# Moving two output evictions to VectorE and easing the first convolution steps in a fused conv + squared-ReLU MLP kernel

## The chip, the core and the metric

The kernel runs on one core of a Trainium2 chip. The metric is the device time of one execution in microseconds (us), the median of several runs. PE is the matrix engine (TensorE), with PEld for its weight loads; DVE is VectorE, ACT is ScalarE, POOL is GpSimd, and SP is the engine that issues nearly all DMAs.

## The reference

The input is `x` of 8 sequences, 4096 tokens each, 192 features. A causal convolution of 7 taps per head (8 heads, 24 features each), with softmaxed taps, is followed by an MLP with a squared ReLU. The tokens of all sequences stand in one row of 32768.

```python
w = softmax(weight, axis=-1)                       # 8 heads x 7 taps
out = einsum('hk,bskhg->bshg', w, x_unf)           # causal, 6 zeros ahead of each sequence
h = out @ w_in                                     # 192 -> 2048
g = s * maximum(h, 0)**2 + b
y = g @ w_out                                      # 2048 -> 192
```

Weights arrive as 64-bit floats; the kernel keeps each operand as a high and a low 32-bit part (fp32r), so one product becomes three matmuls: high by high, high by low, low by high.

## The kernel before

**Tiling.** Tokens are cut into 32 superblocks `n` of 1024, each of two blocks `j` of 512. The 2048 hidden features are 8 pairs `p` of 256. A step `(n, j, p)` computes one pair for one block: `first` (L522) makes `h`, 18 matmuls on 64 rows each; `relu` and `square` (L543, L551) run on ACT; a cast to `qh` (L554) and a subtraction to `ql` (L559) run on DVE; `second` (L604) adds 20 matmuls into four accumulators. Matmuls on the upper and the lower 64 rows stand in turn, so that two of them can run side by side. The finished `qh`, `ql` wait in `queue`, so that `second` runs two steps behind `first` (LAG = 2). When a block's eighth pair is done, its sums are evicted (L634 and L637 on ACT, L638, L642 and L647 on POOL).

**Superblock 0** is different. There the two blocks run side by side while the weights are still being widened, `second_whole` (L569) uses all 128 rows, and its eviction (L585 to L593) makes `oA` (128 features) on ACT, `oC` (64 features) on ACT and `oB` from `oC` on DVE. `oC` has one buffer, so that the second block's `oC` waits for the first block's `oB`.

**Tokens.** The features that a superblock needs are prepared by a `Tokens` object (L130) as a chain of 28 parts: for block 0 the seven taps of features A (L161, L163 on DVE), a copy on ACT (L178), a subtraction on DVE with the swap of halves by two DMAs (L180, then L171 and L172 into `wA`); then the seven taps of features B for both blocks at once, `hiB` (L191), and one part per block of L195 and L196 on DVE into `tB`. Behind the second of these parts `swap` sends `tB` to `wB` by two DMAs. Last come the nine parts of features A of block 1. `first` reads `sA`, then `tB` and `wB`, then `wA`.

**Who does parts when.** `convolve(k)` (L708) does the next k parts of the coming tokens. It stops at the last tap of a convolution, and parts that are not done then are `owed` to the next call. In superblock 1, block 0, each step calls `convolve(3)`; in block 1, which also does the column sums for the bias (L494 to L500), `convolve(1)`; in superblock 2 three and two in turn; from superblock 3 on two. `finish` (L261) completes at the start of a block what its first step cannot do without. Behind the first step of superblock 2, `biases` (L506) makes the bias with four small matmuls (L512).

**What sets the order.** Superblock 0 is traced with `in_order`, which keeps the written order on DVE, ACT and PE. Behind that a scheduler places the instructions of each engine by priority and by its own estimate of when they are ready, and each engine then runs its list strictly in that order. `convolve` runs `behind` the DVE and ACT instructions traced before it.

Of the kernel before, what the change touches and what calls it, by code (L numbers as in the profile page):

```python
# [13 lines left out]
AF = mybir.ActivationFunctionType  # L14
ALU = mybir.AluOpType
# [22 lines left out]
def conv_attention_then_squared_relu_mlp(  # L38
# [23 lines left out]
    nc = tc.nc  # L62
# [15 lines left out]
    sb = const.tile([P, 1], F32, name="sb")  # L78
# [29 lines left out]
    def behind(*engines):  # L108
        return last_of(*engines)()
# [168 lines left out]
    def w_outA(part, f, rows=slice(0, P)):  # L278
        return W[rows, f // 2, part, CI + f % 2 * P :][:, 0:P]

    def w_outB(f, rows=slice(0, P)):
        return WB[rows, f // 2, f % 2, :]
# [196 lines left out]
    def column_sums(k):  # L479

        nonlocal sumA, sumB
        if k == 1:
            free = wordp.tile([P, CT, 2], I32, name="words").bitcast(F32)
            free = free.rearrange("p f w -> p (f w)")
            sumA = free[:, 0 : 4 * P].rearrange("p (h c) -> p h c", h=2)
            sumB = free[:, 4 * P : 4 * P + 5 * DB]
            nc.gpsimd.memset(sumB[:, 0:DB], 0.0)
        for o, w in (
            (sumA, W[:, k, :, CI:CB]),
            (sumB[:, DB:].rearrange("p (j d) -> p j d", j=2), WB[:, k, :, :]),  # L490
        ):
            before = W[:, 0, :, CI:CB] if o is sumA else WB[:, 0, :, :]
            before = before.bitcast(F32) if k == 1 else o
            nc.vector.tensor_tensor(o, before, w.bitcast(F32), op=ALU.add)  # L494
        if k == NPAIR - 1:
            a, b = sumA, sumB[:, DB:]
            nc.vector.tensor_tensor(a[:, 0, :], a[:, 0, :], a[:, 1, :], op=ALU.add)
            nc.vector.tensor_tensor(a[:, 0, 0:P], a[:, 0, 0:P], a[:, 0, P:], op=ALU.add)
            nc.vector.tensor_tensor(b[:, 0:P], b[:, 0:P], b[:, P:], op=ALU.add)
            nc.vector.tensor_tensor(b[:, 0:DB], b[:, 0:DB], b[:, DB:P], op=ALU.add)  # L500
# [5 lines left out]
    def biases():  # L506

        pb = ps_h.tile([P, 2, BLK], F32, name="h")
        for k, cols in enumerate((sumA[:, 0, 0:P], sumB[:, 0:P])):
            for i in range(2):  # L510
                r = slice(i * HB, (i + 1) * HB)
                nc.tensor.matmul(pb[:, i, k : k + 1], cols[r], bb[r], start=True, stop=True)  # L512
        nc.scalar.copy(bias[:, 0:2], pb[:, 0, 0:2])
        nc.vector.tensor_tensor(bias[:, 0:2], bias[:, 0:2], pb[:, 1, 0:2], op=ALU.add)
        nc.vector.tensor_copy(bias[0:DB, 2:3], bias[DB:P, 1:2])
        for o, to, k in unbiased:
            rows = slice(0, o.shape[0])
            nc.gpsimd.tensor_scalar(o, o, bias[rows, k : k + 1], None, op0=ALU.add)
            nc.sync.dma_start(to, o)


    def first(n, j, p, meanwhile=None):  # L522
        h = ps_h.tile([P, 2, BLK], F32, name="h")
        halves = [tok[n].half(j, i) for i in range(2)]

        def both(w, part, at, start, stop):

            for i in range(2):
                chunk = halves[i][at]
                rows = slice(i * HB, (i + 1) * HB)  # L530
                nc.tensor.matmul(  # L531
                    h[:, i, :], w_in(w, p, chunk[0], rows), chunk[part], start=start, stop=stop
                )

        for at in (0, 2, 1):
            both(0, 1, at, at == 0, False)
            both(0, 2, at, False, False)
            both(1, 1, at, False, at == 1)
            if meanwhile and at == 0:
                meanwhile()  # L540
        return h
# [6 lines left out]
    def squares(h, cast):  # L548
        return square(relu(h), cast)
# [7 lines left out]
    def lows(q, qh):  # L557
        ql = qs.tile([P, 2, BLK], F32R, name="ql")
        nc.vector.tensor_tensor(ql, q, qh.bitcast(F32), op=ALU.subtract)  # L559
        return qh, ql  # L560
# [3 lines left out]
    def accumulators(n, j, p):  # L564
        if p == 0:
            acc[n, j] = [ps_o.tile([P, BLK], F32, name=f"acc{k}") for k in (1, 2, 1, 2)[: 4 if n else 2]]
        return acc[n, j]

    def second_whole(n, j, p, qh, ql):  # L569


        a1, a2 = accumulators(n, j, p)
        for i in range(2):
            f = 2 * p + i
            st, sp = f == 0, f == NF - 1
            nc.tensor.matmul(a2, w_outB(f), qh[:, i, :], start=st, stop=False)  # L576
            nc.tensor.matmul(a2, w_outB(f), ql[:, i, :], start=False, stop=sp)  # L577
        for i in range(2):
            f = 2 * p + i
            st, sp = f == 0, f == NF - 1  # L580
            nc.tensor.matmul(a1, w_outA(1, f), qh[:, i, :], start=st, stop=False)  # L581
            nc.tensor.matmul(a1, w_outA(0, f), qh[:, i, :], start=False, stop=False)  # L582
            nc.tensor.matmul(a1, w_outA(0, f), ql[:, i, :], start=False, stop=sp)  # L583
        if p == NPAIR - 1:
            t0 = n * SUP + j * BLK  # L585
            oA = outs.tile([P, BLK], F32, name="oA")
            nc.scalar.activation(oA, a1, AF.Identity, scale=sb)
            oC = outs.tile([DB, BLK], F32, name="oC", bufs=1)
            nc.scalar.activation(oC, a2[DB:P, :], AF.Identity, scale=sb[DB:P])  # L589
            oB = outs.tile([P, BLK], F32, name="oB")[0:DB]  # L590
            nc.vector.scalar_tensor_tensor(
                oB, a2[0:DB, :], sb[0:DB], oC, op0=ALU.mult, op1=ALU.add
            )  # L593
            unbiased.append((oA, outT[0:P, t0 : t0 + BLK], 0))
            unbiased.append((oB, outT[P:D, t0 : t0 + BLK], 2))
            del acc[n, j]
# [100 lines left out]
    def start_tokens(n):  # L697
        if n < NSUP:
            tok[n] = Tokens(n)
            tok[n].load()  # L700
# [7 lines left out]
    def convolve(k):  # L708


        k += owed[0]
        with behind(nc.vector, nc.scalar):
            while k and coming[0] in tok:
                try:
                    stop = next(tok[coming[0]].todo)
                except StopIteration:
                    coming[0] += 1
                    continue
                k -= 1
                if stop:  # L720
                    break
        owed[0] = k if coming[0] in tok else 0
# [38 lines left out]
    with in_order(nc.vector, nc.scalar, nc.tensor):  # L761
        with in_order(nc.sync):
            head()
        headed = last_of(nc.sync)
        for p in range(NPAIR):
            if p > 1:
                if p + 3 < NPAIR:
                    with headed():
                        fetch(p + 3)
                pair(p)  # L770
            if p > 0 and p not in TWICE:
                while len(queue) > (LAG if p < NPAIR - 1 else 0):
                    second_whole(*queue.pop(0))
# [3 lines left out]
    for n, j, p in steps:  # L777
        if p == 0:
            tok[n].finish(j)
            if j == 0:  # L780
                with headed():
                    start_tokens(n + 1)
            else:
                tok.pop(n - 1)
        with begun() if n == 1 else ExitStack():
            h = first(n, j, p)
            queue.append((n, j, p, *lows(*squares(h, nc.vector.tensor_copy))))
        if (n, j) == (1, 1):
            if p < NPAIR - 1:
                with behind(nc.vector):  # L790
                    column_sums(p + 1)
            convolve(1)
        elif p < NPAIR - 1 or n == 1:

            convolve(3 if n == 1 else 3 - p % 2 if n == 2 else 2)
        if (n, j, p) == (2, 0, 0):
            biases()


        while queue and len(queue) > LAG + (queue[0][2] == 0 and queue[0][:2] != (1, 0)):  # L800
            item = queue.pop(0)
            (second if item[0] else second_whole)(*item)
# [46 lines left out]
```

## Time and profile before

| | us |
|---|---|
| median of 3 runs | 2234.77 |
| range of the runs | 2234.75 to 2234.77 |
| span of the profiled execution | 2232.9 |
| PE busy in it | 2226.4 |
| of it without PE in the first 32 us | 1.55 |
| of it without PE from 2225 to the end | 4.5 |
| DVE busy | 1753.5 |
| ACT busy | 1286.4 |
| POOL busy | 317.8 |

The profile is one execution; its span runs from the first to the last instruction, and the medians above hold some 1.9 us more that lies around the span. Its own time beside the runs is that span. A matmul on 64 rows is shown as lasting 386 ns, but two of them run side by side and the next pair starts before the last has ended, so that positions are read from start to start: a step of superblock 1 or later takes 4.31 us on PE. The granted TensorE clock of the execution is 1.000 of 2.4 GHz.

### The profile page before, as it was taken

To read this page: it belongs to the slowest core of one execution; us is meant where nothing else is said; L and a number is where in the kernel's file an instruction comes from. 1 tells how busy PE (TensorE), PEld (TensorE's weight loads), DVE (VectorE), ACT (ScalarE), POOL (GpSimd) and SP (SyncE) were. 2 spreads that over 40 slices of the span, in tenths; PEclk is the share of its full clock that TensorE was granted. 3 is DMA by queue.
4 is the path that set the end of the run, shared out by engine and by line. 5 is a ranking of instruction groups with operands and counts; after the bars stand their busy time and mean duration, and the time that the engine had idled before them with its cause. 6 is when DMAs were issued, how large, how long until landed. Compare 5 with 4: busy or idle time off the path is not lost.

```text
span 2232.9 us, 45081 instructions
## 1 busy us (share of the span) xinstructions
PE 2226.4 (100%) x19330; PEld 1829.1 (82%) x19330; DVE 1753.5 (79%) x1995; ACT 1286.4 (58%) x1410; POOL 317.8 (14%) x205
## 2 busy tenths in 40 slices
PE   9999999999999999999999999999999999999999
PEld 6788888888888888888888888888888888888887
DVE  8898778777787787777877878778777787787764
ACT  8755555655555555555555555555655555556554
POOL 0022101111011011110110111111101111011110
PEclk9999999999999999999999999999999999999999
DMA  5113112121121111211111111112121121111110
GB/s 180 34 43 87 40 46 62 48 58 44 44 58 53 53 44 45 56 53 53 43 51 50 53 53 53 48 43 62 51 55 44 44 58 53 53 44 42 46 39 17
DMA packets 46168, 117.51 MB, mean 53 GB/s; under 512 B 7760, under 2 KB 8016, under 8 KB 45968
## 3 DMA queue, kind: packets, MB, share of 16 engines
q1 hardware_dynamic: 45824, 114.50, 18.6%
q8 instruction: 151, 2.47, 0.5%
q14 instruction: 49, 0.40, 0.1%
q10 hardware_dynamic: 144, 0.13, 0.0%
HBM read 31.64 MB, written 25.17 MB: 25 GB/s over the span
## 4 chain that ended last, share of the span: by engine, by line
PE 98%; DVE 1%; ACT 1%; DMA 0%; issue 0%; SPq 0%; DVEq 0%
PE acc L614 50%; PE h L531 46%; DVE accA L163 0%; PE acc L576 0%; ACT q L552 0%; DVE ql L559 0%; PE acc L577 0%; PE acc L583 0%; PE acc L582 0%; PE acc L581 0%; ACT qh L554 0%; ACT q L545 0%; DMA xA<-in_xA 0%; DVE t L315 0%; ACT oC L589 0%
## 5 line engine op out<-in xcount | busy, mean ns | idle before, releaser
L545 ACT ACTIVATE q<-h 128x1024 f32<-128x1024 f32 x512 | 525.5, 1026 | 902.8 <-PE h L531 900.4
L559 DVE TENSOR_TENSOR ql<-q,qh 128x1024 fp32r<-128x1024 f32 x512 | 656.7, 1283 | 56.3 <-ACT qh L554 2.6
L554 DVE CAST qh<-q 128x1024 fp32r<-128x1024 f32 x497 | 370.1, 745 | 395.7 <-ACT q L552 393.3
L614 PE MATMUL acc<-qh,W 64*128 64x512 f32 x3960 | 609.9, 386 | 0.0
L552 ACT ACTIVATE q<-q 128x1024 f32<-128x1024 f32 x512 | 543.6, 1062 | 15.9
L614 PEld LDWEIGHTS acc<-qh,W 64*128 64x128 f32 x3960 | 370.9, 184 | 77.9
L531 PE MATMUL h<-sA,W 64*128 64x512 f32 x3072 | 432.4, 387 | 0.0
L531 PE MATMUL h<-wA,W 64*128 64x512 f32 x3072 | 431.6, 386 | 0.0
L531 PE MATMUL h<-tB,W 64*128 64x512 f32 x1536 | 429.9, 386 | 0.0
L531 PE MATMUL h<-wB,W 64*128 64x512 f32 x1536 | 429.9, 386 | 0.0
L614 PE MATMUL acc<-ql,WB 64*128 64x512 f32 x1980 | 385.7, 386 | 0.4 <-DVE ql L559 0.4
L614 PE MATMUL acc<-qh,WB 64*128 64x512 f32 x1980 | 385.6, 386 | 0.0
L614 PE MATMUL acc<-ql,W 64*128 64x512 f32 x1980 | 385.5, 386 | 0.0
L638 POOL TENSOR_TENSOR oB<-oB,oB 128x512 f32<-128x512 f32 x61 | 115.2, 1889 | 1672.7 <-ACT oB L637 1672.7
L163 DVE SCALAR_TENSOR_TENSOR accA<-xA,tap,accA 128x512 f32<-128x512 f32 x378 | 341.5, 903 | 6.8
L531 PEld LDWEIGHTS h<-sA,W 64*128 64x128 f32 x3072 | 287.3, 184 | 62.9 <-issue 1.1
L531 PEld LDWEIGHTS h<-wA,W 64*128 64x128 f32 x3072 | 287.8, 184 | 60.4
L531 PEld LDWEIGHTS h<-tB,W 64*128 64x128 f32 x1536 | 282.6, 184 | 40.5 <-issue 0.2
L531 PEld LDWEIGHTS h<-wB,W 64*128 64x128 f32 x1536 | 282.5, 184 | 20.1
L614 PEld LDWEIGHTS acc<-ql,WB 64*128 64x128 f32 x1980 | 185.5, 184 | 40.1 <-DVE ql L559 1.3
L614 PEld LDWEIGHTS acc<-ql,W 64*128 64x128 f32 x1980 | 185.5, 184 | 39.0
L614 PEld LDWEIGHTS acc<-qh,WB 64*128 64x128 f32 x1980 | 185.5, 184 | 38.8
(115 smaller groups left out, 1035.4 us busy)
## 6 DMA issues: line engine op xcount, KB each, us to landing
wA<-sA SPq DMA_DIRECT2D x126, 256.0 KB, 3.6
outT<-oA SPq DMA_DIRECT2D x63, 256.0 KB, 2.0
wB<-tB SPq DMA_DIRECT2D x60, 256.0 KB, 3.4
xA<-in_xA SPq DMA_DIRECT2D x24, 515.0 KB, 3.6
xB<-in_xB SPq DMA_DIRECT2D x32, 259.0 KB, 2.6
oC<-oB SPq DMA_DIRECT2D x61, 128.0 KB, 2.2
outT<-oC SPq DMA_DIRECT2D x60, 128.0 KB, 2.3
words<-in_w SPq DMA_DIRECT2D x7, 768.0 KB, 6.2
```

Of the source, the lines that this page charges most:

```text
L163: nc.vector.scalar_tensor_tensor(acc, src, w[:, k : k + 1], acc, op0=ALU.mult, op1=ALU.add)
L531: nc.tensor.matmul(h[:, i, :], w_in(w, p, chunk[0], rows), chunk[part], start=start, stop=stop)
L545: nc.scalar.activation(q, h, AF.Relu)
L552: nc.scalar.activation(q, q, AF.Square)
L554: cast(qh, q)
L559: nc.vector.tensor_tensor(ql, q, qh.bitcast(F32), op=ALU.subtract)
L614: nc.tensor.matmul(accs[to + 2 * i], w(f, r), q[r, f % 2, :], start=start and f == 0, stop=stop and f == ends[i],)
L638: nc.gpsimd.tensor_tensor(o[1], o[1], o[3], op=ALU.add)
```

## The change

Two edits. In `second_whole`, `oA` of both blocks of superblock 0 is computed by DVE (`tensor_scalar`, out of the accumulator) in place of ACT. In superblock 1, block 0, the first step asks `convolve` for 0 parts and the second for 2, where each asked for 3.

```diff
@@ -584,7 +584,7 @@
         if p == NPAIR - 1:
             t0 = n * SUP + j * BLK
             oA = outs.tile([P, BLK], F32, name="oA")
-            nc.scalar.activation(oA, a1, AF.Identity, scale=sb)
+            nc.vector.tensor_scalar(oA, a1, sb, None, op0=ALU.mult)
             oC = outs.tile([DB, BLK], F32, name="oC", bufs=1)
@@ -792,7 +792,8 @@
         elif p < NPAIR - 1 or n == 1:
 
-            convolve(3 if n == 1 else 3 - p % 2 if n == 2 else 2)
+            ahead = (0, 2) if n == 1 else ()
+            convolve(ahead[p] if p < len(ahead) else 3 if n == 1 else 3 - p % 2 if n == 2 else 2)
```

The first condition above this branch is `(n, j) == (1, 1)`, so the two smaller numbers hold for block 0 of superblock 1 alone. Everything behind them moves by the parts that were not done.

**DVE from the end of superblock 0 on.** `acc_376` and `acc_388` are the features-A sums of blocks 0 and 1, `acc_377` and `acc_389` their features-B sums. Before:

```order
L216 TENSOR_TENSOR wB<-accB,hiB 64x512
L591 SCALAR_TENSOR_TENSOR oB<-acc_377,sb,oC 64x512
L591 SCALAR_TENSOR_TENSOR oB<-acc_389,sb,oC 64x512
L554 CAST qh<-q 128x1024
L559 TENSOR_TENSOR ql<-q,qh 128x1024
L216 TENSOR_TENSOR tB<-accB,hiB 64x512
L161 TENSOR_SCALAR accA<-xA,tap 128x512
L163 SCALAR_TENSOR_TENSOR accA<-xA,tap,accA 128x512 x2
```

Now:

```order
L216 TENSOR_TENSOR wB<-accB,hiB 64x512
L587 TENSOR_SCALAR oA<-acc_376,sb 128x512
L591 SCALAR_TENSOR_TENSOR oB<-acc_377,sb,oC 64x512
L587 TENSOR_SCALAR oA<-acc_388,sb 128x512
L591 SCALAR_TENSOR_TENSOR oB<-acc_389,sb,oC 64x512
L554 CAST qh<-q 128x1024
L559 TENSOR_TENSOR ql<-q,qh 128x1024
L216 TENSOR_TENSOR tB<-accB,hiB 64x512
```

The two evictions stand between those that DVE did before, and the taps L161 and L163 that followed L216 stand one step later.

**DVE at the end of superblock 1**, in steps (1,1,6) and (1,1,7), from the last of the column sums (L500) to the bias (L514). Before:

```order
L500 TENSOR_TENSOR words<-words 128x64
L163 SCALAR_TENSOR_TENSOR accA<-xA,tap,accA 128x512
L554 CAST qh<-q 128x1024
L559 TENSOR_TENSOR ql<-q,qh 128x1024
L514 TENSOR_TENSOR bias<-bias,h 128x2
```

Now:

```order
L500 TENSOR_TENSOR words<-words 128x64
L195 CAST tB<-accB 64x512
L196 TENSOR_TENSOR tB<-accB,hiB 64x512
L554 CAST qh<-q 128x1024
L559 TENSOR_TENSOR ql<-q,qh 128x1024
L514 TENSOR_TENSOR bias<-bias,h 128x2
```

Before, L163 stands once more between L559 and L514; now L195 and L196 stand there once more, for block 1. The features B of superblock 2 are thus split in the last two steps of superblock 1, four steps later than before, and the swap into `wB` follows the second pair.

**PE in the first step of superblock 2**, `first(2,0,0)` with the bias matmuls (L512) and `second(1,1,6)` (L614), each with the semaphore that it waits for (DMAHW is a DMA, DVE and Activation are engines). Before:

```order
L531 MATMUL h<-tB,W 128x512
L531 MATMUL h<-wB,W 128x512 [waits DMAHW7_49]
L531 MATMUL h<-wB,W 128x512 [waits DMAHW0_49]
L531 MATMUL h<-tB,W 128x512 x2
...
L531 MATMUL h<-wA,W 128x512 x4
L512 MATMUL h<-bb,words 128x1 [waits DVE_49,Activation_49]
...
L614 MATMUL acc_1515<-qh,WB 128x512
```

Now:

```order
L531 MATMUL h<-tB,W 128x512 [waits DVE_49]
L512 MATMUL h<-bb,words 128x1 [waits Activation_49]
...
L614 MATMUL acc_1504<-qh,WB 128x512
...
L614 MATMUL acc_1504<-ql,WB 128x512
L531 MATMUL h<-wB,W 128x512 [waits DMAHW7_49]
L614 MATMUL acc_1506<-ql,WB 128x512
...
L614 MATMUL acc_1503<-ql,W 128x512
L531 MATMUL h<-wB,W 128x512 [waits DMAHW0_49]
L531 MATMUL h<-tB,W 128x512 [waits DVE_49]
...
L531 MATMUL h<-wA,W 128x512 x4
L614 MATMUL acc_1505<-ql,W 128x512
```

The first seven matmuls of `second(1,1,6)` now stand ahead of the first matmul that reads `wB`, six more ahead of the second one, and the last seven behind the end of `first(2,0,0)`. This is the only place where the order of PE differs. From superblock 3 on, DVE runs one part behind where it stood before: a step that held L191 and one pair of L195 and L196 now holds L191 and both pairs, with a lighter step ahead of it.

## Rows read from the trace of the kernel before

**Rows 1.** Span and granted clock; then one window: its length, busy us (instructions), PEclk, DMA.

```profile
core 0: 2232.9 us, clock 1.000
...
106.30:1200.00 1093.70, 1093.70 (x9656) 903.96 (x9654) 871.66 (x982) 619.62 (x669) 166.35 (x104) 1.00 0.19 52
```

**Rows 2.** Timeline, superblock 1's start: start us, us, engine, line, operation, count, [idle, releaser].

```profile
91.54 0.69 ACT L587 ACTIVATE oA<-acc,sb 128x512 f32<-128x512 f32 x1
91.55 0.74 DVE L591 SCALAR_TENSOR_TENSOR oB<-acc,sb,oC 64x512 f32<-64x512 f32 x1 [1.32 <-ACT oC L589]
92.32 0.69 ACT L589 ACTIVATE oC<-acc,sb 64x512 f32<-64x512 f32 x1
92.37 0.85 PE L531 MATMUL h<-sA,W 64*128 64x512 f32 x6
93.03 1.02 ACT L545 ACTIVATE q<-h 128x1024 f32<-128x1024 f32 x1
95.91 1.23 DVE L559 TENSOR_TENSOR ql<-q,qh 128x1024 fp32r<-128x1024 f32 x1
96.45 0.39 PE L614 MATMUL acc<-qh,WB 64*128 64x512 f32 x2
97.19 0.50 PE L614 MATMUL acc<-ql,WB 64*128 64x512 f32 x2 [0.35 <-DVE ql L559]
99.36 0.84 PE L531 MATMUL h<-sA,W 64*128 64x512 f32 x6
100.59 1.23 DVE L559 TENSOR_TENSOR ql<-q,qh 128x1024 fp32r<-128x1024 f32 x1
104.05 0.84 PE L531 MATMUL h<-sA,W 64*128 64x512 f32 x6
```

**Rows 3.** Timeline, the last B part and its swap in the kernel before, step (1,1,3).

```profile
143.29 0.42 DVE L195 CAST tB<-accB 64x512 fp32r<-64x512 f32 x1
143.74 0.46 SPq L172 DMA_DIRECT2D wB<-tB  x1
144.46 0.46 SPq L171 DMA_DIRECT2D wB<-tB  x1
144.47 0.70 DVE L554 CAST qh<-q 128x1024 fp32r<-128x1024 f32 x1
146.41 0.69 DVE L494 TENSOR_TENSOR words<-words,W 128x512 f32<-128x512 f32 x1
```

**Rows 4.** Those two DMAs, L172 then L171, by line; then all 64 into wB.

```profile
DMA to landing us min/median/max: 3.1/3.1/3.1
...
DMA to landing us min/median/max: 3.5/3.5/3.5
...
DMA to landing us min/median/max: 2.2/3.3/4.7
```

**Rows 5.** Timeline, the first step of superblock 2.

```profile
155.27 0.74 DVE L163 SCALAR_TENSOR_TENSOR accA<-xA,tap,accA 128x512 f32<-128x512 f32 x1
156.41 0.39 PE L531 MATMUL h<-tB,W 64*128 64x512 f32 x1
157.77 0.50 PE L512 MATMUL h<-bb,words 64*128 64x1 f32 x8
158.13 0.48 PE L614 MATMUL acc<-qh,WB 64*128 64x512 f32 x2
160.54 0.84 PE L531 MATMUL h<-sA,W 64*128 64x512 f32 x6
```

**Rows 6.** Timeline, steady state: step (n,1,2) in a later superblock.

```profile
413.61 1.22 DVE L559 TENSOR_TENSOR ql<-q,qh 128x1024 fp32r<-128x1024 f32 x1
416.90 0.39 PE L614 MATMUL acc<-ql,WB 64*128 64x512 f32 x2
```

**Rows 7.** Groups by form in the first 18 us: line, operation, shape, count | busy us, mean ns.

```profile
L257 PE MATMUL acc<-xB,q 128*128 128x512 f32 x14 | 6.2, 596 | 0.0
L388 PE MATMUL acc<-q 128*128 128x512 f32 x2 | 2.1, 1142 | 1.0 <-POOL xA L145 1.0
```

## The prediction

> **What bounds the kernel now.** I read the busy times first: PE works in 2226.4 of 2232.9 us, with a granted clock of 1.000, the full 2.4 GHz, and behind 106.3 us without any gap (the order of the window's columns is PE, PEld, DVE, ACT, POOL) [rows 1]. So an edit on ACT or DVE pays only where PE waits for them. Of the 6.5 us without PE, 1.55 lie in the head and 4.5 in the tail, behind the last matmuls; the change touches neither. The second view was the timeline where superblock 1 begins. There `second(1,0,0)` puts its first `qh` pair on PE at 96.45 and its first `ql` pair only at 97.19, released by the DVE subtraction L559 that ran from 95.91 to 97.14; a second L559 ends at 101.82 and holds `second(1,0,1)` in the same way [rows 2]. These two are the waits that the change can take away. The third view was the timeline at the first step of superblock 2, where PE runs without a gap from 156.41 to 160.54 [rows 5], and the fourth the DMAs that carry `tB` to `wB` [rows 3, 4]; the order of the changed kernel shows that these two meet.
>
> **The rate of PE.** From the matmul at 156.41 to the bias at 157.77 there are 12 matmuls in 1.36 us [rows 5]: 0.113 us each when two row halves stand in turn, 0.227 a pair. A `first` of 18 is then 2.04 us, a `second` of 20 is 2.27, and a step 4.31.
>
> **Part 1, what the two waits are worth.** From 96.45 to 99.36 PE spends 2.91 us on a `second` that costs 2.27: 0.64 lost. From 99.36 to 104.05 it spends 4.69 on a step of 4.31: 0.38 lost [rows 2]. The most that can come back is 1.02 us. Behind them PE has no gap [rows 1].
>
> *The evictions.* ACT did `oA`, `oC`, `oA`, `oC` ahead of the first L545, 0.71 us apart, so from about 90.12 on, and L545 started at 93.03 [rows 2]. Without the two `oA` the first `oC` ends at 90.8. DVE now does `oA` ahead of its L591. No row shows this operation on DVE. One-input work on 512 columns takes 0.42 us (L195) [rows 3], the two-input L591 takes 0.74 us from an accumulator [rows 2]; I take 0.74, because L591 reads what `oA` reads, and 0.42 as the other end. PE ends the sums of block 1 near 90.25, block 0's are done before, so the first `oA` runs to about 91.0, the first `oB` to 91.75, the second `oC`, which waits for it, to 92.45. L545 cannot start before `first(1,0,0)` is through, and the next `first` started at 92.37 [rows 2], so its result is there at about 92.55. L545 thus comes 0.45 earlier than 93.03, limited by PE and no longer by ACT; with 0.42 for `oA` the limit is the same. The first L559 then ends at 97.14 - 0.45 = 96.69 where PE asks for it at 96.45 + 0.23 = 96.68. The 0.64 is gone but for about 0.07.
>
> *The smaller numbers.* Between the two subtractions DVE did L216 and three taps. The taps now stand a step later, which takes some 2 us out from ahead of the second L559, and the 0.38 is gone too. I take **0.95 us** back; the ends are 0, if a new wait takes the place of the old, and 1.02.
>
> *What is late instead.* Four parts fewer are done, and everything behind stands four parts later. The parts of superblock 1's own block 1 end one step later, some 4 us, and `first(1,1,0)` that reads them comes at about 121: covered by several us. The loads that SP issues behind released buffers (`xA`, `xB`) move behind the output DMAs, but they fetch a superblock ahead: nothing. The B split of superblock 2 has no such cover.
>
> **Part 2, the swap in front of superblock 2.** In the kernel before, the last B part began at 143.29 in step (1,1,3), and `first(2,0,0)` read `wB` at about 156.6: 13 us of cover. Now the same part is the last thing of step (1,1,7), and the cover is gone. I place it on the clock of before. DVE's first pair L195, L196 stands where L163 started, at 155.27 [rows 5]. From there to the next cast is 144.47 - 143.29 = 1.18 us, and through cast and subtraction 146.41 - 144.47 = 1.94 [rows 3]: the second pair starts at 155.27 + 3.12 = 158.39. SP issued L172 0.45 and L171 1.17 behind the start of that pair [rows 3]: 158.84 and 159.56. These two DMAs took 3.1 and 3.5 us to land [rows 4]: 161.94 and 163.06. The 64 into `wB` lie between 2.2, which are the half-sized ones, and 4.7 [rows 4]; I take the pair's own.
>
> PE reaches the first `wB` matmul early: 156.41, plus 0.23 for the single `tB` matmul, plus 0.36 for the bias (157.77 to 158.13), plus seven matmuls of `second(1,1,6)` at 0.33 (the first pair is slower there) + 0.23 + 0.23 + 0.23 [rows 5]: 158.02. It waits until 161.94, **3.92 us**. Behind that stand this matmul, alone since the next is on the same rows, and six more: 0.23 + 3 x 0.23 = 0.91, to 162.85, and the second `wB` matmul waits 0.21 for L171, to 163.06. Ten matmuls end `first(2,0,0)` at 164.2, seven end `second(1,1,6)` at 165.0, and the next `first` can pair with the last of them, so 164.95 where it was 160.54 [rows 5]: **4.4 us** later. Of this 4.13 is waiting, the rest matmuls whose partner on the other rows is missing. The scheduler's filling is counted: without the thirteen matmuls moved forward the wait would be longer. Nothing hides the rest, since PE's list is strict. ACT and DVE idle meanwhile and start behind it with less backlog than before; POOL's six bias additions follow L514, which is late by 0.3 us at most.
>
> **Part 3, the steady state.** One step of each later superblock holds L191 and both pairs of L195 and L196, in place of L191 and one pair. That is one pair more, 1.18 us [rows 3]; the step ahead is lighter by about that. L559 ended at 414.83 where PE asked at 416.90: 2.1 us of slack [rows 6]. I cost it at nothing; if the pair fell into POOL's work, which stretches DVE, it might take twice as long and would still fit.
>
> **The sum.** 2232.9 - 0.95 + 4.4 = 2236.4 us of span, so with the 1.87 us around it 2238.2, or 3.45 us (0.15%) above the median of 2234.77. Some 0.2%, 4.47 us, is what a measurement of this kernel can tell from no change, so 2238.2 counts as the same, though close to its edge at 2239.2. Ends: the gain 0 to 1.02; the DMAs 0.4 earlier to 1 later. This gives 2237.4 to 2240.1 on its own.
>
> **The rivals.**
>
> *PE's clock falls in the wait (slower).* The longest idle stretch of PE between head and tail is the 0.35 us at 97.19, and the clock is granted in full [rows 1, 2]; the new one is 3.9 us, and no row shows what PE does after such a one. At the very start, after no work at all, a matmul of 128x512 took 1142 ns where the same shape took 596 ns a little later, with the granted clock still shown as 1.000 [rows 1, 7]. Half speed for as long as those two matmuls lasted, 2.1 us [rows 7], would cost 1 us, for four times that 4 us; I take twice, 4.2 us, so 2.1 lost: 2238.2 + 2.1 = 2240.3, with ends at 2239.2 and 2242.4. It decides by the length of the gap: 0.35 us leaves the clock alone, and if it falls only in a gap of more than 3.9 us nothing happens. The Trainium skill ("TensorE: Matmul & The Clock Gate", section "HAM oscillation — how this bites in real kernels") says that an engine idle for too long between bursts restarts at half clock; no run here shows it, and the time would be the one just given.
>
> *The swap is hidden after all (no wait).* If DVE is ahead of PE there and the pair starts some us earlier than I place it, the wait shrinks by the same. For: DVE's load in block 1 is smaller now. Against: the cast between the two pairs needs ACT's square of (1,1,7), and with it PE's own position, so that not much over 1 us can be won. Without any wait: 2233.8; with 1 us won: 2237.2.
>
> *A step of every superblock overruns (slower).* From 2.1 us more than I count, each of some 29 superblocks would lose the excess: 0.2 us each is 5.8 us, 2244. The lighter step ahead speaks against it.
>
> *The change does not do what it says.* DVE's `oA` sits in front of `oB`, on which the second `oC` waits; were it to take over 1.2 us, L545 would be as late as before. The taps' part of the gain stays: 2238.8.
>
> **How the numbers follow.** The forecast, a wait of about 4 us at the full clock: 0.60. The clock falls: 0.20. A wait shorter by over 1 us: 0.13. The steady state: 0.04. Evictions no help: 0.03, inside the forecast's range. The range reaches from the shorter wait to the fallen clock, 2236.0 to 2241.5. Slower by over 0.2% are the fallen clock, the steady state and the upper end of the forecast: 0.20 + 0.04 + 0.08 = 0.32. Faster by over 0.2% would need 4.47 us, of which the waits hold 1.02: 0.01. The same: 0.67.
>
> **What would show it.** Right: no `ql` wait left in `second(1,0,0)`; L587 on DVE near 0.7 us; PE waiting once for about 3.9 us at a `wB` matmul of `first(2,0,0)`, released by the DMA; 34.45 us from block to block behind it as before. Wrong: 64-row matmuls longer than 386 ns behind the wait (the clock), a wait under 3 us, or PE waiting again in the blocks behind.

## The result, and the profile of the changed kernel

The changed kernel takes **2240.26 us** (median of 12 runs, 2239.70 to 2241.38) against 2234.82 us of the kernel before on the same chip (2234.46 to 2235.05): a ratio of 1.0025, 95% interval 1.0017 to 1.0033. It is slower by 5.44 us, 0.24%. That lies inside the range that was forecast, 2.1 us above its centre and just beyond the 0.2% up to which "the same" was to go. The time is that of the rival in which PE's clock falls in the new wait.

The runs with a mean granted clock of 0.999 took 2239.70 to 2240.42 us, those with 0.998 took 2240.56 to 2241.38. Only the slowest of them was profiled (2241.38 us), so that its loss is read 1.1 us larger than the median's.

The span and the granted clock, which was 1.000 in [rows 1]:

```profile
core 0: 2239.6 us, clock 0.998
```

The one wait of PE that is new, from the view of waits (us in total, times, longest):

```profile
PE h L531 <- DMA wB<-tB: 3.9, 1, 3.9
```

Where PE stands idle and at which clock, by windows (length, busy us of PE, PEld, DVE, ACT, POOL with their counts, PEclk, DMA share, GB/s):

```profile
160.00:161.00 1.00, 0.00 (x0) 0.00 (x0) 0.00 (x0) 0.00 (x0) 1.00 (x2) 0.69 0.90 193
161.00:167.00 6.00, 5.45 (x26) 4.34 (x28) 0.00 (x0) 1.18 (x2) 6.00 (x4) 0.50 0.47 156
167.00:168.00 1.00, 1.00 (x12) 0.81 (x10) 0.07 (x1) 0.90 (x1) 1.00 (x2) 0.90 0.34 76
...
170.00:1200.00 1030.00, 1030.00 (x9092) 851.27 (x9090) 801.10 (x905) 585.11 (x630) 162.95 (x94) 1.00 0.19 52
1200.00:2190.00 990.00, 990.00 (x8738) 818.23 (x8736) 758.21 (x853) 562.23 (x605) 153.79 (x90) 1.00 0.18 49
```

Two losses stand behind each other: a wait of 3.9 us, and some 6.8 us at the lower of the two clock levels, 1.2 GHz. From 161.55, where PE works again, to 167.2 are 5.65 us of work at half rate, which at 2.4 GHz would have been 2.8. Behind 168 PE is busy in every microsecond at the full clock, with as many matmuls in each window as before (8738 in the second one in both kernels). The first of the two windows in the kernel before:

```profile
170.00:1200.00 1030.00, 1030.00 (x9090) 851.27 (x9090) 811.89 (x902) 582.40 (x628) 150.27 (x96) 1.00 0.19 52
```

**The head of superblock 1**, in the timeline (start us, us, engine, line, operation, count, [idle, releaser]):

```profile
90.42 0.69 ACT L589 ACTIVATE oC<-acc,sb 64x512 f32<-64x512 f32 x1
90.44 0.74 DVE L587 TENSOR_SCALAR oA<-acc,sb 128x512 f32<-128x512 f32 x1
90.52 0.97 PE L531 MATMUL h<-sA,W 64*128 64x512 f32 x6
91.98 0.69 ACT L589 ACTIVATE oC<-acc,sb 64x512 f32<-64x512 f32 x1 [0.87 <-DVE oB L591]
92.92 1.03 ACT L545 ACTIVATE q<-h 128x1024 f32<-128x1024 f32 x1 [0.25 <-PE h L531]
95.79 1.23 DVE L559 TENSOR_TENSOR ql<-q,qh 128x1024 fp32r<-128x1024 f32 x1
96.80 0.39 PE L614 MATMUL acc<-qh,WB 64*128 64x512 f32 x2
97.07 0.19 PEld L614 LDWEIGHTS acc<-ql,WB 64*128 64x128 f32 x2 [0.31 <-DVE ql L559]
97.08 0.50 PE L614 MATMUL acc<-ql,WB 64*128 64x512 f32 x2
99.25 0.84 PE L531 MATMUL h<-sA,W 64*128 64x512 f32 x6
103.56 0.84 PE L531 MATMUL h<-sA,W 64*128 64x512 f32 x6
```

In [rows 2] L545 stood behind ACT's evictions; here it waits for PE. The `ql` pair comes 0.28 us behind the `qh` pair (0.74 there), though its weight load (PEld) still waits 0.31 us for L559, and the next step takes 4.31 us (4.69 there). In the kernel before `first(1,0,0)` started at 90.17; from there to the matmul at 104.05 are 13.88 us, here 103.56 - 90.52 = 13.04. The change gives back **0.84 us**. (The start itself is 0.35 us later in this profile: the head's matmuls took longer, and the change touches none of them.)

**The swap in front of superblock 2** in the timeline, with DVE, SP's queue and PE:

```profile
157.30 0.39 PE L614 MATMUL acc<-ql,WB 64*128 64x512 f32 x1
157.97 0.42 DVE L195 CAST tB<-accB 64x512 fp32r<-64x512 f32 x1
158.42 0.46 SPq L172 DMA_DIRECT2D wB<-tB  x1
159.14 0.46 SPq L171 DMA_DIRECT2D wB<-tB  x1
161.55 0.79 PE L531 MATMUL h<-wB,W 64*128 64x512 f32 x1 [3.86 <-DMA wB<-tB]
163.00 0.62 PE L531 MATMUL h<-wB,W 64*128 64x512 f32 x1
166.41 0.62 PE L531 MATMUL h<-sA,W 64*128 64x512 f32 x1
```

The two DMAs, by line of the tile `wB`:

```profile
DMA to landing us min/median/max: 3.1/3.2/3.4
```

Where [rows 3] have this cast at 143.29, it now starts at 157.97, and its two DMAs land 3.1 and 3.4 us behind their issue (3.1 and 3.5 in [rows 4]). Matmuls that last 0.39 us elsewhere last 0.62 here, at the granted clock of 0.50.

### The profile page after: what moved, and what is told of

Same layout as the page of the kernel before. It is cut to its first block, busy times and chain, and to the rows that moved or that the text cites. A ratio compares the mean times of both kernels' runs of the same rounds, so it can differ in the third digit from the quotient of the medians.

```text
span 2239.6 us, 45098 instructions
## 1 busy us (share of the span) xinstructions
PE 2230.3 (100%) x19330; PEld 1831.9 (82%) x19330; DVE 1727.6 (77%) x1997; ACT 1288.4 (58%) x1408; POOL 337.8 (15%) x205
## 4 chain that ended last, share of the span: by engine, by line
PE 99%; DVE 0%; DMA 0%; ACT 0%; issue 0%; DVEq 0%; POOL 0%; POOLq 0%
PE acc L614 50%; PE h L531 47%; PE acc L257 1%; PE acc L576 0%; PE acc L577 0%; PE acc L583 0%; PE acc L582 0%; PE acc L581 0%; PE acc L388 0%; DMA wB<-tB 0%; DVE ql L559 0%; DVE qh L554 0%; ACT q L552 0%; ACT q L545 0%; DVE words L494 0%
## 5 line engine op out<-in xcount | busy, mean ns | idle before, releaser
L545 ACT ACTIVATE q<-h 128x1024 f32<-128x1024 f32 x512 | 526.1, 1027 | 902.0 <-PE h L531 899.8
L614 PE MATMUL acc<-qh,W 64*128 64x512 f32 x3960 | 860.9, 387 | 0.0
L559 DVE TENSOR_TENSOR ql<-q,qh 128x1024 fp32r<-128x1024 f32 x512 | 664.1, 1297 | 55.5 <-ACT qh L554 2.6
L614 PEld LDWEIGHTS acc<-qh,W 64*128 64x128 f32 x3960 | 632.8, 184 | 78.2
L614 PE MATMUL acc<-ql,W 64*128 64x512 f32 x1980 | 676.2, 386 | 0.0
L531 PE MATMUL h<-sA,W 64*128 64x512 f32 x3072 | 650.0, 387 | 0.0
L531 PE MATMUL h<-wA,W 64*128 64x512 f32 x3072 | 649.8, 387 | 0.0
L614 PE MATMUL acc<-ql,WB 64*128 64x512 f32 x1980 | 570.0, 386 | 0.0
L614 PE MATMUL acc<-qh,WB 64*128 64x512 f32 x1980 | 569.4, 386 | 0.0
L531 PE MATMUL h<-wB,W 64*128 64x512 f32 x1536 | 509.1, 387 | 3.9 <-DMA wB<-tB 3.9
L531 PEld LDWEIGHTS h<-sA,W 64*128 64x128 f32 x3072 | 460.8, 184 | 63.0 <-issue 1.5
L531 PEld LDWEIGHTS h<-wA,W 64*128 64x128 f32 x3072 | 461.6, 184 | 60.6
L531 PE MATMUL h<-tB,W 64*128 64x512 f32 x1536 | 508.1, 386 | 0.0
L614 PEld LDWEIGHTS acc<-ql,W 64*128 64x128 f32 x1980 | 359.8, 184 | 39.1
L163 DVE SCALAR_TENSOR_TENSOR accA<-xA,tap,accA 128x512 f32<-128x512 f32 x378 | 341.7, 904 | 6.8
L531 PEld LDWEIGHTS h<-tB,W 64*128 64x128 f32 x1536 | 282.5, 184 | 40.5 <-issue 0.2
L614 PEld LDWEIGHTS acc<-ql,WB 64*128 64x128 f32 x1980 | 272.6, 184 | 39.2 <-DVE ql L559 0.3
L614 PEld LDWEIGHTS acc<-qh,WB 64*128 64x128 f32 x1980 | 272.4, 184 | 38.8
L531 PEld LDWEIGHTS h<-wB,W 64*128 64x128 f32 x1536 | 282.9, 184 | 24.5 <-DMA wB<-tB 4.3
```

What stands on the lines that cost most here:

```text
L163: nc.vector.scalar_tensor_tensor(acc, src, w[:, k : k + 1], acc, op0=ALU.mult, op1=ALU.add)
L531: nc.tensor.matmul(h[:, i, :], w_in(w, p, chunk[0], rows), chunk[part], start=start, stop=stop)
L545: nc.scalar.activation(q, h, AF.Relu)
L614: nc.tensor.matmul(accs[to + 2 * i], w(f, r), q[r, f % 2, :], start=start and f == 0, stop=stop and f == ends[i],)
```

## The experiments

The theory: the whole loss is the swap, which now ends in step (1,1,7); it costs a wait, and the wait costs the clock. The evictions and the taps at the head are harmless and give back 0.84 us. The rivals: the evictions on VectorE, or the later superblocks, carry a part of the loss; and the slow matmuls behind the wait come from something other than PE's standing idle. The kernel before took 2234.84 to 2234.89 us (median) beside all of these.

### Each half of the change alone

The evictions alone:

```diff
-            ahead = (0, 2) if n == 1 else ()
+            ahead = ()
```

> VectorE does the two features-A evictions of superblock 0, and the steps of superblock 1 do as many parts of the convolution as before. Theory (the whole loss is PE's wait for wB in first(2,0,0) and the low clock behind it; the evictions are harmless): the first ql wait is gone, the second stays, since the taps stand where they stood, and the B split stays in step (1,1,3), so no wB wait and no lower clock: some 0.5 us faster than before, 2234.3. Rival (the oA on VectorE costs something by itself, or the changed eviction leaves ACT and VectorE worse off behind it): no gain, 2235 or more.

The parts alone:

```diff
-            nc.vector.tensor_scalar(oA, a1, sb, None, op0=ALU.mult)
+            nc.scalar.activation(oA, a1, AF.Identity, scale=sb)
```

> The other half alone: the two evictions are on ACT as before, and superblock 1's first two steps do 0 and 2 parts. Theory: the wB wait of 3.9 us in first(2,0,0) and the stretch at half clock behind it are there in full, the first ql wait of 0.35 stays, the second is gone: some 0.4 us above the changed kernel, 2240.7 (2240.0 to 2241.9), by about 6 us slower than before. Rival (the loss needs the evictions on VectorE): 2234 to 2235, no wB wait.

The evictions alone: **2234.39 us**, ratio 0.9998 (0.9989 to 1.0006). The interval does not tell that from the kernel before, but the trace tells where it is gained: from 90.47 to 103.86 are 13.39 us, 0.49 less than the 13.88 of before. The parts alone: **2241.61 us**, ratio 1.0029 (1.0018 to 1.0039), a bit above what was expected, with a mean clock of 0.998 in five of its seven runs. Its head takes 104.06 - 90.52 = 13.54, 0.34 less than before. The timeline of the parts alone:

```profile
97.56 0.50 PE L614 MATMUL acc<-ql,WB 64*128 64x512 f32 x2 [0.38 <-DVE ql L559]
104.06 0.84 PE L531 MATMUL h<-sA,W 64*128 64x512 f32 x6
162.02 0.79 PE L531 MATMUL h<-wB,W 64*128 64x512 f32 x1 [3.83 <-DMA wB<-tB]
```

The first `ql` wait belongs to the evictions and the second to the taps, 0.49 and 0.34, together 0.83 of the 0.84. The wait at `wB` is there in full with all the evictions on ACT. The rival that VectorE's evictions cost something falls.

### All four parts given back (repaid)

```diff
-            ahead = (0, 2) if n == 1 else ()
+            ahead = (0, 2, 4, 4, 4, 4) if n == 1 else ()
```

> The changed kernel, but the four parts that the first two steps leave out are done by the four steps behind them (parts per step 0, 2, 4, 4, 4, 4, then 3): the B split of superblock 2 ends in the steps around (1,1,3) again. Theory: both ql waits are gone as in the changed kernel, no wB wait, clock 1.000: 0.85 us faster than before, 2234.0, and 6.3 us faster than the changed kernel. Rival (the loss comes from the order of the first superblock or from each later superblock): it stays at 2238 or more.

Measured **2233.89 us** (2233.52 to 2234.43), ratio to the kernel before 0.9996 (0.9987 to 1.0005): by the medians 0.95 us faster than before and 6.4 us faster than the changed kernel. Its clock is 1.000, and its `wB` matmuls follow `tB` at once:

```profile
155.10 0.84 PE L531 MATMUL h<-sA,W 64*128 64x512 f32 x6
155.78 0.39 PE L531 MATMUL h<-tB,W 64*128 64x512 f32 x1
155.78 0.61 PE L531 MATMUL h<-wB,W 64*128 64x512 f32 x2
159.91 0.84 PE L531 MATMUL h<-sA,W 64*128 64x512 f32 x6
```

So the whole loss, and nothing of the gain, hangs on the four late parts. Giving them back puts the later superblocks back into their old order too (DVE is busy for 812.5 us from 170 to 1200, as before, where the changed kernel has 801.1), so this run alone does not clear them. The windows of the changed kernel do: PE has no gap there and as many matmuls as before. This kernel is the best of those run, though its lead over the kernel before is smaller than its interval can settle; that both waits are gone, its trace shows (13.03 us from `first(1,0,0)` to the matmul at 103.42).

### The length of the wait

In one kernel (repaid1) one part is given back, so that the split ends a step earlier:

```diff
-            ahead = (0, 2) if n == 1 else ()
+            ahead = (0, 2, 4) if n == 1 else ()
```

In the other (early) the last pair of the split stands ahead of the cast of step (1,1,7):

```diff
+        if (n, j, p) == (1, 1, 7):
+            convolve(1)
         with begun() if n == 1 else ExitStack():
             h = first(n, j, p)
...
             if p < NPAIR - 1:
                 with behind(nc.vector):
                     column_sums(p + 1)
-            convolve(1)
+                convolve(1)
```

> The changed kernel with one part given back: superblock 1's third step does 4 parts, so three parts are late and the B split of superblock 2 ends in step (1,1,6), its last pair a step of VectorE earlier; PE's list puts wB right behind tB there. Estimate from the profile: PE waits some 2.2 us for wB and 0.9 for the second DMA. At the full clock 2237.0; if the clock falls in the gap too, 2239.5. Theory without the clock (the loss is the wait alone) gives the first as well, so the granted clock behind the wait decides.

> As many late parts as the changed kernel, but in step (1,1,7) the last pair of the B split is issued ahead of that step's cast and subtraction, so its two DMAs leave some 2 us of VectorE time earlier; the DMA takes as long. PE's list puts wB right behind tB, with nothing to fill the wait. Estimate: a wait of about 3.3 us for wB and 0.8 for the second DMA. At the full clock 2238.1, with the clock fallen behind it 2240.6 or a little more.

Measured **2240.14 us** (2237.34 to 2240.77), ratio 1.0022 (1.0013 to 1.0031), and **2241.47 us** (2240.83 to 2241.93), ratio 1.0030 (1.0018 to 1.0041). The waits in the timeline of repaid1:

```profile
158.47 0.50 PE L531 MATMUL h<-wB,W 64*128 64x512 f32 x1 [2.13 <-DMA wB<-tB]
159.54 0.79 PE L531 MATMUL h<-wB,W 64*128 64x512 f32 x1 [0.57 <-DMA wB<-tB]
```

and in that of early:

```profile
155.31 0.84 PE L531 MATMUL h<-sA,W 64*128 64x512 f32 x6
159.57 0.49 PE L531 MATMUL h<-wB,W 64*128 64x512 f32 x1 [3.19 <-DMA wB<-tB]
160.61 0.69 PE L531 MATMUL h<-wB,W 64*128 64x512 f32 x1 [0.56 <-DMA wB<-tB]
```

The waits are close to what was expected (2.2 and 0.9; 3.3 and 0.8), while the times lie 0.6 and 0.9 us above what was expected with the clock fallen. But the shorter wait of repaid1 did not save the clock: its time is 0.1 us below the changed kernel's, where its waiting is 1.2 us less (2.70 against 3.86). Its fastest run, 2237.34 us, lies near the 2237.0 that the wait alone was to cost; the others, from 2238.97 on, took 1.6 to 3.4 us longer than that one.

### The clock alone

PE is kept busy through the two waits of each of those kernels by matmuls whose weights are the constant tile `gap`, set to zero, which add nothing to the sums: 28 and 5 in early, 19 and 5 in repaid1.

```diff
...
                 chunk = halves[i][at]
                 rows = slice(i * HB, (i + 1) * HB)
+                fill = {(0, 1, 2, 0): 28, (0, 2, 2, 0): 5}.get((w, part, at, i), 0)
+                for k in range(fill if (n, j, p) == (2, 0, 0) else 0):
+                    r = slice(k % 2 * HB, (k % 2 + 1) * HB)
+                    nc.tensor.matmul(
+                        h[:, k % 2, :], gap[r, 0:P], tok[n].sA[0][r, 0, :], start=False, stop=False
+                    )
```

> The kernel called early (the changed kernel with the last pair of the B split ahead of the cast of its step), with PE kept busy through its two waits: 28 matmuls ahead of the tB matmul and 5 between the two wB matmuls, with zeros as weights, added into the same accumulator, so that no sum changes. Nothing else moves on PE, ACT or VectorE, and wB lands when it did, so the delay of first(2,0,0) by the DMA is the same. Theory (the clock falls because PE stood idle): granted clock 1.000 throughout, no matmul of 64 rows over 0.5 us behind the wait. In the profile of early the half clock lasted 6.8 us, 6.6 of them with work, so 3.3 us come back: 2238.2 against the 2241.5 of early. Rival (the slow matmuls come from the DMA's late data, or the clock falls anyway): no faster than early, 2241 or more.

> The same for the kernel called repaid1 (three late parts in place of four): 19 zero matmuls ahead of the tB matmul and 5 between the two wB matmuls fill its waits of 2.1 and 0.6 us. Theory: the granted clock stays at 1.000 and the half clock's share comes back, 3.3 us in the profile of repaid1 and less in its faster runs: 2237.2 (2236.9 to 2237.5), within the 2237.0 that the wait alone was to cost. With early_fill it gives the price of the wait alone at two lengths, about 1 us apart. Rival: no faster than the 2240.1 of repaid1.

Measured **2238.49 us** (2238.32 to 2239.56), ratio 1.0017 (1.0007 to 1.0026), and **2237.43 us** (2237.14 to 2237.70), ratio 1.0011 (1.0002 to 1.0021). The same stretch by windows, of early:

```profile
160.00:161.00 1.00, 0.45 (x3) 0.39 (x4) 0.00 (x0) 0.00 (x0) 0.00 (x0) 0.88 0.00 0
161.00:167.00 6.00, 6.00 (x34) 4.86 (x34) 2.07 (x4) 2.11 (x3) 2.58 (x2) 0.50 0.00 0
167.00:168.00 1.00, 1.00 (x9) 0.77 (x7) 0.99 (x2) 0.00 (x0) 1.00 (x1) 0.71 0.69 262
```

and of early with its waits filled:

```profile
160.00:161.00 1.00, 0.91 (x10) 0.55 (x8) 0.00 (x0) 0.00 (x0) 0.00 (x0) 1.00 0.00 0
161.00:167.00 6.00, 6.00 (x60) 4.99 (x58) 3.26 (x6) 2.49 (x4) 3.81 (x2) 1.00 0.12 46
```

The step in the timeline of early with its waits filled (where L531 has become L538):

```profile
155.04 0.84 PE L538 MATMUL h<-sA,W 64*128 64x512 f32 x6
160.36 0.49 PE L538 MATMUL h<-wB,W 64*128 64x512 f32 x1
164.38 0.84 PE L538 MATMUL h<-sA,W 64*128 64x512 f32 x6
```

In the same six microseconds, busy throughout, PE does 34 matmuls at the clock of 0.50 and 60 at 1.00 (the eight short ones of the bias among both). The data come no earlier: from the first `sA` matmul of `first(2,0,0)` to the second `wB` matmul are 5.32 us with the waits filled (155.04 to 160.36) and 5.30 without (155.31 to 160.61). So the DMA is not what makes the matmuls slow; PE's standing idle is. The clock alone costs 2241.47 - 2238.49 = **2.98 us** at the longer wait and 2240.14 - 2237.43 = **2.71 us** at the shorter. What is left above the kernel with all parts given back, 4.60 and 3.54 us, is the waits (3.75 and 2.70) and 0.85 us, alike in both. Nearly all of it lies in this one step: from its first `sA` matmul to that of the next `first` are 4.81 us in repaid (155.10 to 159.91) and 9.34 in early with its waits filled, 4.53 more. The 0.85 is put down to matmuls whose partner on the other rows is missing; no run separates it. The Trainium skill ("TensorE: Matmul & The Clock Gate", section "HAM oscillation — how this bites in real kernels") says that PE restarts at half clock after it has waited too long between bursts; these two pairs agree, and the shorter wait, 2.13 us, lies below the idle gaps that the section warns of, where the measurement decides.

### Another order, with and without work in the wait (hoist, hoist_fill)

The changed kernel with `second(1,1,6)`, the head of the queue, whole ahead of the `tB` and `wB` matmuls, and the same with 26 zero matmuls behind it:

```diff
+    def second_before():
+        second(*queue.pop(0))
...
-        with begun() if n == 1 else ExitStack():
-            h = first(n, j, p)
+        with begun() if n == 1 else in_order(nc.tensor) if (n, j, p) == (2, 0, 0) else ExitStack():
+            h = first(n, j, p, second_before if (n, j, p) == (2, 0, 0) else None)
```

> The changed kernel with PE's order at first(2,0,0) fixed: second(1,1,6) stands whole ahead of the tB and wB matmuls, so all ten matmuls of first behind the wait stand together; the bias columns come behind. PE then falls idle near 158.5 on the changed kernel's clock and waits until 161.6 for wB: 3.0 us instead of 3.9, and some 0.6 for the second DMA. If the clock falls in this wait as well: 2239 to 2240.5, with matmuls at 0.6 us and a granted clock of 0.5 behind it. If a wait of this length leaves the clock alone: about 2237.6, all matmuls at 0.39 or less, mean clock 1.000.

> As hoist, with 26 more matmuls (2.9 us of PE time) between second(1,1,6) and the tB matmul: zeros as weights, added into the same accumulator, so they change no sum and only keep PE busy while the DMA lands. wB is awaited as long as in hoist. Theory (clock): the granted clock stays at 1.000 and everything behind the wait runs at the full rate: 2237.4 to 2238, faster than hoist by what the half clock costs there, 1.5 to 3 us. Rival (the long matmuls behind the wait come from the DMA or from the operands, not from idleness): no faster than hoist.

Measured **2243.51 us** (ratio 1.0038, 1.0023 to 1.0053) and **2242.20 us** (1.0033, 1.0020 to 1.0046). On the clock they say what the other pairs say: the mean is 0.998 or 0.999 in every run without filling, the fall stands behind the wait in the profiled one, and the mean is 1.000 in every run with filling. On the price they say less, since both took longer than expected (2240.5 and 2238 at most) and run into waits that the changed kernel does not have. In the first, from the timeline of DVE, POOL and PE:

```profile
174.15 1.99 POOL L518 TENSOR_SCALAR oB<-oB,bias 64x512 f32<-64x512 f32 x1
176.12 1.97 POOL L638 TENSOR_TENSOR oB<-oB,oB 128x512 f32<-128x512 f32 x1
174.75 2.18 DVE L559 TENSOR_TENSOR ql<-q,qh 128x1024 fp32r<-128x1024 f32 x1
180.52 1.57 POOL L647 TENSOR_TENSOR oC<-oC,oB 64x512 f32<-64x512 f32 x1 [0.72 <-DMA oC<-oB]
180.98 2.19 DVE L559 TENSOR_TENSOR ql<-q,qh 128x1024 fp32r<-128x1024 f32 x1
183.22 0.50 PE L614 MATMUL acc<-ql,WB 64*128 64x512 f32 x2 [1.55 <-DVE ql L559]
```

The bias columns now stand behind the wait, so POOL's six bias additions (L518) start at 165.29 instead of 159.40 and run beside DVE's work instead of in its idle time. L559 beside POOL takes 2.19 us, alone 1.22 [rows 6], and PE waits 1.55 us for the second of them. The filled kernel has the same wait (its L566 is this subtraction) and one more, for an eviction on ACT:

```profile
173.69 0.49 PE L621 MATMUL acc<-qh,WB 64*128 64x512 f32 x1 [0.99 <-ACT oB L644]
182.67 0.50 PE L621 MATMUL acc<-ql,WB 64*128 64x512 f32 x2 [1.50 <-DVE ql L566]
```

What is left of the excess in either was not traced.

## Why the prediction came out as it did

**The gain: right in place, 0.84 instead of 0.95.** Both waits went, for the two reasons given, 0.49 to the evictions and 0.34 to the taps. The first was the mis-sized term: 0.57 of 0.64 was to come back, but `second(1,0,0)` still takes 2.45 us (96.80 to 99.25) instead of 2.27. The forecast had L559 end when PE reaches the `ql` matmul, and it does (97.02 and 97.03); what it left out is that the weights of that matmul are loaded ahead of it, and this load waited 0.31 us for L559.

**The evictions: right.** L587 took 0.74 us on DVE, the value taken from L591's row, and L545 was limited by PE. That they do not help falls as a rival.

**The wait: right.** Forecast 3.92 us at a `wB` matmul of `first(2,0,0)`, released by the DMA; measured 3.86. The pair that was placed at 158.39 started at 157.97, the first DMA was to land at 161.94 and PE went on at 161.55; both differences are about the 0.84 of gain less the 0.35 of the later head. The landing times 3.1 and 3.5 us became 3.1 and 3.4. The second wait, 0.21 us for L171, did not show: at half clock PE came to that matmul at 163.00, when the data had landed. The rival in which the swap stays hidden falls with it. Too small, it seems, was the remainder, 0.27 us for matmuls whose partner on the other rows is missing: the two filled kernels leave 0.85 that no wait explains, though in another order of PE.

**The steady state: right.** It was costed at nothing, and behind 168 us the changed kernel has no gap and does as many matmuls in the same windows as the kernel before.

**The clock: the step that failed.** The forecast let the clock stay at 1.000 and gave the fall 0.20 of the chance. The reason put forward was that the only gap on record, 0.35 us, leaves the clock alone, and that the fall "decides by the length of the gap". Nothing in the rows lay between 0.35 and 3.9 us, so the length spoke for neither side, while [rows 7] showed that PE is slow after standing idle: 1142 ns for a matmul that takes 596 a little later. That row, and the rule named beside it, should have weighed more than the clock's 1.000 in a kernel whose PE hardly stood idle. The runs put in its place: waits of 2.13, 2.98, 3.19, 3.83 and 3.86 us all let the clock fall in the profiled run, and filled waits did not.

One longer idle stretch was on record, the tail of the kernel before, and it would have misled: PE does nothing from 2228.4 to the end of the span, and the clock stays at 1.00. In the tail of the kernel with the evictions alone it falls 2.1 us after the last matmul, which ends at 2228.2. By windows, the kernel before and then that one:

```profile
2229.00:2232.90 3.90, 0.00 (x0) 0.00 (x0) 0.47 (x2) 0.00 (x0) 0.00 (x0) 1.00 0.38 101
```

```profile
2230.00:2231.00 1.00, 0.00 (x0) 0.00 (x0) 0.00 (x0) 0.00 (x0) 0.00 (x0) 0.65 0.94 265
```

So a single idle stretch at 1.00 does not show that its length is harmless, and a mean clock of 0.999 can come from the tail alone.

**The size of that rival: about right.** It was priced at 2.1 us (ends 1.0 and 4.2), for a low clock of 4.2 us, and with 2240.3 as its time. The low clock of the profile lasted 6.8 us and cost 2.8, so the term was sized too short there; the pairs gave 2.71 and 2.98. At the full clock the changed kernel would take some 2238.6 us (an estimate: 2233.89 of repaid, 3.86 of wait and 0.85 for missing partners), so the median, 2240.26, holds 1.7 us of it. The sum of the waits was nearly right, and the time was not.

## What to carry to other kernels

Work that is taken off the front of a strict list does not vanish: follow it to the step where it is done now, and look at what its last DMA released there; here four parts moved back by a few steps turned 13 us of cover into a wait of 3.9. Price a new idle stretch of PE twice, once for its length and once for the clock behind it, which here was another 2.71 and 2.98 us in the two pairs. If parts have to be left out of busy steps, give them back within the next few steps, ahead of the one with the transfer.

## What the runs showed of the hardware

- The granted clock fell to 0.50 for some 6.8 us in the profile of the changed kernel (from about 160.4 to 167.2), and as long with the early pair. A shorter wait did not mean a smaller fall: with waits of 2.13 and 0.57 us it still cost 2.71 by the medians, though the fastest of those ten runs, 2237.34 us, paid next to nothing for it (the filled kernel took 2237.43).
- The clock can fall when PE is already at work again. In hoist PE waited 2.98 us until 161.31 and 0.56 until 162.37 at a granted clock of 1.00, and the clock fell behind that, with PE busy, for a shorter time, some 3.4 us; by windows:

```profile
163.00:164.00 1.00, 1.00 (x14) 0.81 (x10) 0.00 (x0) 0.07 (x1) 0.00 (x0) 0.78 0.00 0
164.00:166.00 2.00, 2.00 (x14) 1.72 (x16) 0.30 (x2) 2.00 (x3) 0.71 (x1) 0.50 0.04 8
166.00:167.00 1.00, 1.00 (x8) 0.81 (x6) 0.89 (x2) 0.04 (x1) 1.00 (x1) 0.52 0.00 0
```

- DVE's subtraction L559 took 2.18 and 2.19 us beside POOL's work and 1.22 alone. An overlap does not always stretch DVE: at 166.80 in hoist L559 took 1.22 beside POOL's L518, and it was the L518 begun at 167.21 that took 2.25 us, where one took 1.55 alone (at 160.95 in the changed kernel). The Trainium skill ("SBUF — State Buffer", section "Who interferes with whom") has a VectorE instruction with two inputs in SBUF contend with a GpSimd instruction that reads it, which these rows agree with; it has one of the two wait whole, while at 174.75 in hoist both took longer than alone (L518 1.99), and which of them waited can't be read from the spans on POOL.
